# Raw token tiles through the first query and key projections, normalised at the eviction

## The chip, the cores and the metric

The kernel runs on one core of one Trainium2 chip. The metric is the device time of one execution in microseconds (us); lower is better. The core has a matrix engine (PE, whose weight loads are listed as PEld), a vector engine (DVE), a scalar engine (ACT), GpSimd (POOL) and a queue engine (SP) that starts transfers. Transfers run on 16 DMA engines.

## The reference, cut to what matters

```
h  = x + A(layernorm(x))          # attention with a compressive memory, 32 heads of 32
h2 = h + B(layernorm(h))          # gated MLP, 1024 -> 3584 -> 1024
layernorm(x) = (x - mean(x)) / sqrt(var(x) + 1e-5)      # over the 1024 features, no weights
A: q, k, v = n @ wq, n @ wk, n @ wv        # n = layernorm(x), 2048 tokens x 1024
   four segments of 512 tokens; in each: causal softmax attention, plus a read of the memory
   that the earlier segments left; output @ wo
```

All data are bf16. For a token t and an output column o of wq or wk the projection can be written in two ways, which are equal apart from rounding:

```
sum_d (x[t,d] - mean[t]) * r[t] * w[d,o]  =  (sum_d x[t,d]*w[d,o]  -  mean[t] * sum_d w[d,o]) * r[t]
```

with r[t] = (var[t] + 1e-5)^-0.5. The second form needs the column sum of w once, and mean and r of a token only after the product.

## The kernel before, in words

Tokens are worked on in four segments of 512 (four tiles of 128 tokens), features in 8 chunks of 128. A projection of 128 output columns for a segment is a group of 8 matmuls (one for each chunk) into one PSUM bank; there are 8 banks, 0 to 3 shared with the attention scores, 5 to 7 the usual ones of the dense work.

Each engine runs its instructions in an order that is written out: `ORDER` lists for pe, act, dve, pool and sp the numbers of the operations, counted in the order in which the program creates them. `BANKS` gives the first PSUM bank of each group in the order of creation. A group that takes over a bank waits for all operations of the bank's former group, its eviction among them. Waits are derived from what operations read and write; an engine that waits holds everything behind it in its list. A transfer is an entry of the list of the engine that issues it (`sp` for all of them before the change).

The start of the program is `constants` (line 767 on) and `first_half`, for the first segment and the first half (512 columns) of wq, wk and wv:

- `warm` issues matmuls of zeros, 12 at the very start and 5 later, into a bank that nothing reads.
- The loads go out on SP in the list's order: the four token tiles (the first in two halves), then wk's first 256 columns, wq's first 256 columns in two halves of the features, the second 256 columns of wq and of wk, a tile of the next segment, and wv.
- `first_tile` takes a token tile: statistics on DVE (`ln_stats`) or on DVE and ACT (`ln_both`), the deviation by a power on POOL (L880), the scaling on DVE in two halves (L884), four transposes of 128x128 on PE for each half (L719), and a copy of each half from PSUM into `xnT`, the transposed input, on ACT or DVE (`evac`, L730 and L731).
- The projections of the first 256 columns of wq and wk follow tile by tile: 4 groups x 4 tiles x 8 matmuls of 128 columns (L707), each group evicted once. The second 256 columns of wq and wk (`project`) run over 512 columns at once, as do the four groups of wv.
- `attention` begins with ten score passes (L1079, operation 361 is the first), each over banks 0 to 3 and followed by an exponential of 128x2048 on ACT (L1093). Between the passes PE works on projections, those of this segment first and then those of the second half.

Later segments are normalised on the chip and transposed by transposing DMAs (`dma_t`, L395) that SP issues.

Of the kernel before, what the change touches and what calls it, by code (L numbers as in the profile page):

```python
# [8 lines left out]
ALU = mybir.AluOpType  # L9
# [82 lines left out]
    "act": (  # L92
# [473 lines left out]
class Kernel:  # L566
# [305 lines left out]
    def first_tile(self, t):  # L872
# [9 lines left out]
        for b in range(2):  # L882
# [8 lines left out]
            if t == 0 and b:  # L891
                self.warm(5, [self.g.ops[-1]])
# [598 lines left out]
```

## Time and profile before

| | |
|---|---|
| median of 3 runs | 883.78 us (883.63 to 884.16) |
| the profiled execution, its own time | 884.58 us |
| its span, first to last instruction | 882.9 us |
| PE busy | 871.0 us (99% of the span), 5736 instructions |
| DVE, ACT, POOL busy | 438.8, 301.7, 163.0 us |
| read and written in HBM | 84.94 MB and 9.44 MB |

The profile is of one execution. Busy time of an engine is the time that its instructions cover; matmuls are pipelined, so PE counts as busy from a matmul's start until its result stands. The chain of waits follows the work that ended last back to the start. A timeline row merges neighbouring instructions of one kind and gives their start, the time that they cover, their count and the idle time ahead of them.

### The profile page before, as it was taken

To read this page: it belongs to the slowest core of one execution; us is meant where nothing else is said; L and a number is where in the kernel's file an instruction comes from. 1 tells how busy PE (TensorE), PEld (TensorE's weight loads), DVE (VectorE), ACT (ScalarE), POOL (GpSimd) and SP (SyncE) were. 2 spreads that over 40 slices of the span, in tenths; PEclk is the share of its full clock that TensorE was granted. 3 is DMA by queue.
4 is the path that set the end of the run, shared out by engine and by line. 5 is a ranking of instruction groups with operands and counts; after the bars stand their busy time and mean duration, and the time that the engine had idled before them with its cause. 6 is when DMAs were issued, how large, how long until landed. Compare 5 with 4: busy or idle time off the path is not lost.

```text
span 882.9 us, 13660 instructions
## 1 busy us (share of the span) xinstructions
PE 871.0 (99%) x5736; PEld 397.6 (45%) x5825; DVE 438.8 (50%) x735; ACT 301.7 (34%) x345; POOL 163.0 (18%) x226
## 2 busy tenths in 40 slices
PE   8999999999999999999999999999999999999998
PEld 5443444444444444444444444444444444444445
DVE  5787887876666777745354301322243344231011
ACT  4878675768656655511111000111011111110000
POOL 1544344335242444303000000000000000000000
PEclk9999999999999999999999999999999999999999
DMA  7789938555962627395484411211322322201011
GB/s 226 206 191 219 231 100 228 143 145 160 235 156 81 170 66 173 89 289 156 115 242 93 116 36 30 77 55 54 96 73 64 96 72 59 91 7 48 19 42 42
DMA packets 148956, 105.75 MB, mean 120 GB/s; under 512 B 46368, under 2 KB 134688, under 8 KB 147872
## 3 DMA queue, kind: packets, MB, share of 16 engines
q1 hardware_dynamic: 148896, 104.89, 45.5%
q8 instruction: 46, 0.75, 0.4%
q14 instruction: 14, 0.11, 0.0%
HBM read 84.94 MB, written 9.44 MB: 107 GB/s over the span
## 4 chain that ended last, share of the span: by engine, by line
PE 98%; issue 1%; DMA 1%; ACT 0%; SPq 0%; DVE 0%; DVEq 0%
PE ps L707 91%; PE ps L1079 3%; PE ps L1172 3%; DMA wp<-in_A_wk_dram 1%; PE ps L1000 0%; PE ps L1296 0%; SPq L388 0%; ACT et L1093 0%; PE ps L1165 0%; PE ps L719 0%; DVE t L1372 0%; ACT sg L1369 0%; DVE ob L1401 0%; DVEq L524 0%
## 5 line engine op out<-in xcount | busy, mean ns | idle before, releaser
L707 PE MATMUL ps<-hnT,w1b 128*128 128x512 bf16 x881 | 214.5, 379 | 1.1 <-issue 0.5
L707 PE MATMUL ps<-hnT,w3b 128*128 128x512 bf16 x875 | 210.8, 379 | 1.6 <-issue 0.6
L707 PE MATMUL ps<-w2b,hm 128*128 128x512 bf16 (+2 forms) x934 | 198.0, 367 | 1.0
L1369 ACT ACTIVATE sg<-ps 128x512 bf16<-128x512 f32 x112 | 66.8, 597 | 385.5 <-PE ps L707 384.3
L1372 DVE SCALAR_TENSOR_TENSOR t<-sg,ps 128x512 bf16<-128x512 bf16 x112 | 76.7, 686 | 190.5 <-ACT sg L1369 190.2
L1093 ACT ACTIVATE et<-ps 128x2048 bf16<-128x2048 f32 x80 | 150.1, 1876 | 47.7 <-PE ps L1079 45.8
L707 PEld LDWEIGHTS ps<-w2b,hm 128*128 128x128 bf16 x952 | 90.6, 98 | 103.4 <-issue 0.3
L707 PEld LDWEIGHTS ps<-hnT,w1b 128*128 128x128 bf16 x896 | 86.2, 98 | 105.8 <-issue 5.6
L707 PEld LDWEIGHTS ps<-hnT,w3b 128*128 128x128 bf16 x896 | 86.3, 98 | 105.5 <-issue 3.1
L1102 POOL TENSOR_SCALAR_AFFINE_SELECT et<-et 128x512 bf16<-128x512 bf16 (+1 forms) x96 | 83.2, 878 | 112.3 <-ACT et L1093 112.3
L1377 DVE SCALAR_TENSOR_TENSOR hm<-t,ps 128x512 bf16<-128x512 bf16 x112 | 76.2, 684 | 43.5 <-PE ps L707 41.6
L1401 DVE TENSOR_TENSOR ob<-hr,ps 128x512 bf16<-128x512 bf16 (+2 forms) x34 | 21.9, 655 | 122.4 <-PE ps L707 122.3
L707 PE MATMUL ps<-xnT,wp 128*128 128x512 bf16 (+1 forms) x344 | 59.8, 320 | 1.7 <-DMA wp<-in_A_wk_dram 0.8
L707 PE MATMUL ps<-wo,oT 128*128 128x512 bf16 x244 | 59.6, 380 | 1.2 <-issue 0.8
L707 PE MATMUL ps<-hnT,wp 128*128 128x512 bf16 x249 | 58.6, 380 | 0.8 <-issue 0.6
L1118 DVE TENSOR_TENSOR sum<-sum,et 128x512 bf16<-128x512 bf16 (+1 forms) x64 | 40.5, 641 | 6.1 <-POOL et L1102 3.8
L707 PEld LDWEIGHTS ps<-xnT,wp 128*128 128x128 bf16 x352 | 27.9, 98 | 27.3 <-issue 3.5
L707 PEld LDWEIGHTS ps<-wo,oT 128*128 128x128 bf16 x256 | 23.8, 98 | 29.8 <-issue 3.0
L707 PEld LDWEIGHTS ps<-hnT,wp 128*128 128x128 bf16 x256 | 23.5, 98 | 29.7 <-issue 3.7
L1079 PE MATMUL ps<-qT,kT 32*128 32x128 bf16 (+3 forms) x512 | 31.7, 301 | 0.0
L1341 DVE TENSOR_TENSOR h<-h,ps 128x512 bf16<-128x512 bf16 x32 | 21.7, 680 | 20.0 <-PE ps L707 19.6
L707 PE MATMUL ps<-wp,hnT 128*128 128x512 bf16 x124 | 29.8, 380 | 0.4 <-issue 0.3
(101 smaller groups left out, 567.9 us busy)
## 6 DMA issues: line engine op xcount, KB each, us to landing
w1b<-in_B_w_dram SPq DMA_DIRECT2D x28, 512.0 KB, 4.1
w3b<-in_B_w_dram SPq DMA_DIRECT2D x28, 512.0 KB, 4.0
wp<-in_A_wv_dram SPq DMA_DIRECT2D x8, 1024.0 KB, 5.8
wp<-in_A_wq_dram SPq DMA_DIRECT2D x7, 1024.0 KB, 5.4
wp<-in_A_wk_dram SPq DMA_DIRECT2D x7, 1024.0 KB, 7.6
w2b<-in_B_w_dram SPq DMA_DIRECT2D x7, 1024.0 KB, 5.8
h<-in_A_x_dram SPq DMA_DIRECT2D x16, 256.0 KB, 3.0
h_scr<-h SPq DMA_DIRECT2D x16, 256.0 KB, 3.4
```

What stands on the lines that cost most here:

```text
L707: return [e.matmul(p[0](gr), p[1], p[2], start=p[3], stop=p[4]) for p in part]
L1079: ins.append(e.matmul(self.bank(gr, j, 512 - 128 * kc, off), k[r, g0 + g, 128 * kc:128 * kc + 128], q[r, g0 + g, 128 * kc:512], start=True ...
L1093: return [e.activation(et[:, :, :], src, AF.Exp, scale=self.scale)]
L1102: self.pool_op(lambda e, v=v, pat=pat: e.affine_select(v, v, pattern=pat, compare_op=ALU.is_ge, fill=0.0, base=0, channel_multiplier=-1), ...
L1118: lambda e, gr: [e.tensor_tensor(o, a, b, op=ALU.add) for o, a, b in sums],
L1172: ins.append(e.matmul(self.ps[32 * i:32 * i + 32, b * 512 + c0:b * 512 + c0 + n], lhsT(i, kc, j), rhs(i, j), start=kc == 0 and j == first, ...
L1341: self.g.op("dve", dve_ns(512), lambda e, gr, hs=hs: [e.tensor_tensor(hs, hs, self.bank(gr), op=ALU.add)], reads=[hs], writes=[hs], cls=1, ...
L1369: self.g.op("act", act_ns(512), lambda e, gr, sg=sg: [e.activation(sg, self.bank(gr), AF.Tanh, scale=0.5)], writes=[sg], cls=0, group=gg)
L1372: e.scalar_tensor_tensor(t1, sg, 1.0, self.bank(gr), op0=ALU.add, op1=ALU.mult)], reads=[sg], writes=[t1], cls=0,
L1377: e.scalar_tensor_tensor(dst, t1, 0.5, self.bank(gr), op0=ALU.mult, op1=ALU.mult)], reads=[t1], writes=[dst], cls=0,
L1401: self.g.op("dve", dve_ns(n), lambda e, gr, hs=hs, ob=ob, n=n: [e.tensor_tensor(ob, hs, self.bank(gr, 0, n), op=ALU.add)], reads=[hs], wri ...
```

## The change

Tiles 0 to 2 of the first segment are transposed as they arrive and kept as `xr`, with one more column of ones ahead of the tokens (column 1). Six groups, wq's four and wk's first two, are multiplied over `xr`. With the column of ones a group also gets the column sum of its weights. Two of the groups (wq 0 and 1) go tile by tile, 129, 128 and 128 columns; the other four (wk 0 and 1, wq 2 and 3) go over 385 columns in one pass. Tile 3 is normalised first, as all tiles were before; the six groups' columns of tile 3 are multiplied into two banks of their own.

Mean and deviation of the three tiles stand as one column a statistic (`st32`, 128 tokens on the partitions). `spread_rows` transposes them on DVE, writes them to a scratch in DRAM and reads them back onto all 128 partitions as rows (`rows`, 384 KB in all); both transfers are entries of ACT's list. At the eviction of each of the six groups ACT copies the column sum with a minus (csum), DVE adds mean x csum to the bank (scalar_tensor_tensor, 384 columns), and DVE or POOL multiplies by the deviation (tensor_tensor, 384 columns).

The three raw tiles are also normalised in place and transposed by DMA into `xnT`, for wk's groups 2 and 3 and for wv. The warm matmuls are 4 at the start, three after the first tile's transposes. The loads are ordered anew, and wk's first 256 columns come in two halves.

Numbers of the changed kernel that the text uses. Loads: 13, 14 tile 0; 15 tile 1; 18 tile 2; 19 tile 3; 16, 17 wq's first 256 columns by halves of the features; 20, 21 the same of wk; 22 wq's second 256; 23 wk's second 256; 24 wv. Tile 0: 27, 29 transposes; 28, 30 copies; 34 to 37 statistics; 38 power; 39 scaling; 40 transposing DMA. Tile 1: 41 to 44, 45 to 51, 52, 53, 54. Tile 2: 55 to 58, 59 to 62, 63, 64, 65. 66 transposes the statistics, 67 writes them to DRAM, 68 reads the rows. Tile 3: 70 to 76 statistics and power; 77, 80 scaling; 78, 81 transposes; 79, 82 copies. 88 to 99 wq 0 and 1 by tiles; 100 to 107 the passes of 385 columns (wk 0, wk 1, wq 2, wq 3); 108 to 119 tile 3's columns. Eviction, three operations a group (csum, add, multiply): 120 to 122 wq 0; 123 to 125 wq 1; 126 to 128 wk 0; 129 to 131 wk 1; 132 to 134 wq 2; 135 to 137 wq 3. 138, 139 copy tile 3's columns. 140 to 145 wk 2 and 3; 146 to 157 wv's four groups (155, 156 are the last group's matmuls). 379 is the first score pass, 380 its exponential, 382 the second pass. From operation 128 of the kernel before on, the new number is the old one plus 18.

The first lines of the lists, before and after, and the program text:

```diff
     "pe": (
-        "1 30 33-34 86 84-85 87 45 80 48 82-83 81 88 90 94 91 56 89 59 92 95 93 102 100 98 70 99 "
-        "73 103 96-97 104-105 101 108 106 109 107 125 361 110 119 126 111 364 120 116-117 122 "
+        "1 27 29 31-33 41 55 43 88 57 90 89 91 94 92-93 95 98 100 102 96 99 97 106 104-105 101 78 "
+        "81 107 112 103 108 113 109 114 110-111 155 115-119 156 379 152-153 382 149-150 143 394 "
...
     "act": (
-        "38-40 31 35 63 46 64-65 71 112-113 362 115 365 353 377 124 372 139 382 373 371 136 133 "
+        "28 30 47-49 71 67 72-73 123 68 132 79 126 82 120 129 139 135 138 380 383 371 395 145 154 "
...
     "dve": (
-        "0 24-27 37 29 32 50 41-42 51 44 47 52-53 62 49 55 58 66-67 57 60 69 72 74 114 127 "
+        "0 34-37 60 59 42 61 44 62 46 50-51 56 58 66 70 53 39 74-75 77 64 80 124-125 121 130 122 "
+        "127-128 136 133 157 372 214-216 198 151 206 219 207 199 208 385 200 86 386 222-223 402 "
...
     "sp": (
-        "13-15 17 19-20 16 18 21-22 179 23 187 203 369 195 140 153 186 166 194 202 210 360 356 "
+        "14 13 18 15-17 19-20 22 21 24 65 40 54 213 23 197 205 158 221 387 171 184 212 220 228 "
...
 BANKS = (
-    "3013010101567456755566775656676655656756755567567577657576000000000001247300000000000124"
+    "3023331201105674230165567575566756676565675675556756757765757600000000000124730000000000"
...
+    def raw_tile(self, t):
+
+        x = self.xs[t][:, :]
+        for b in range(2):
+            gr = Group([(0,), (1,), (2,)], safe=True)
+            self.transposes(gr, [(c * 128, self.xs[t][:, 512 * b + c * 128:512 * b + c * 128 + 128])
+                                 for c in range(4)], 2)
+            self.evac(gr, self.xr[:, 4 * b:4 * b + 4, 2 + 128 * t:130 + 128 * t], 512,
+                      lambda v: v[:, 0:512].rearrange("p (k n) -> p k n", k=4),
+                      cls=1, bf=True, engs=("dve", "act"))
...
+        mv = self.st32[:, 2 * t:2 * t + 2]
+        rs, mean, op = self.ln_both(t, x, mv) if t % 2 else self.ln_stats(t, x, 1, mv=mv)
...
+        self.dve_op(lambda e: e.tensor_scalar(x, x, mean, rs, op0=op, op1=ALU.mult), 540.0,
+                    [x, mean, rs], [x], 1, port=True)
+        self.g.dma_t(self.xnT[0][:, :, t * 128:(t + 1) * 128], x, 3)
+
+    def spread_rows(self):
+
+        a, b = self.st32[:, :], self.st32t[:, :]
+        self.dve_op(lambda e: e.transpose(b, a), 180.0, [a], [b], 0)
+        sd = self.sd
+        to = bass.AP(sd.tensor, sd.offset, [[32, 4], [128, 32], [1, 32]])
+        of = sd[0:6, :]
+        src = bass.AP(of.tensor, of.offset, [[0, 128], [1, 768]])
...
+        o.emit = lambda e, g: [e.dma_start(to, b)]
...
+        o.emit = lambda e, g: [e.dma_start(rows, src)]
...
-        for t in range(4):
-            self.first_tile(t)
+        for t in range(3):
+            self.raw_tile(t)
+        self.spread_rows()
+        self.first_tile(3)
...
+        more = [(wq, i, Group([(0,), (1,), (2,), (3,)])) for i in (2, 3)]
+        for c0, n in ((1, 129), (130, 128), (258, 128), (1, 385)):
+            for w, i, gr in work[2:] + more if n > 129 else work[:2]:
                 self.g.stage()
+                self.mms(gr, [(lambda gr, c0=c0, n=n: self.bank(gr, 0, n, c0),
+                               w[:, c, i * 128:(i + 1) * 128], xr[:, c, c0:c0 + n],
+                               c == 0, c == 7, n) for c in range(8)], 5, split=4, eager=True)
+        ends = [Group([(0,), (1,), (2,), (3,)]) for w in (wq, wk)]
...
+        for n, (w, i, gr) in enumerate(work + more):
...
+            self.g.op("act", 186.0, lambda e, gr, cs=cs: [e.activation(
+                cs, self.bank(gr)[:, 1:2], AF.Copy, scale=-1.0)], writes=[cs], cls=1, group=gr)
+            self.g.op("dve", dve_ns(384), lambda e, gr, part=part, cs=cs: [e.scalar_tensor_tensor(
+                part, means, cs, self.bank(gr, 0, 384, 2).rearrange("p (t b) -> p t b", t=3),
+                op0=ALU.mult, op1=ALU.add)], reads=[means, cs], writes=[part], cls=1, group=gr)
+            self.either(lambda e, out=out, part=part: e.tensor_tensor(
+                out, part, scales, op=ALU.mult), 384, 2, [scales, part], [out], 1)
```

By `BANKS` the six groups stand in banks 5 (wq 0), 6 (wq 1), 7 (wk 0), 4 (wk 1), 2 (wq 2) and 3 (wq 3), tile 3's columns in banks 0 and 1, and wv's last group (155) takes bank 5.

## Rows read from the trace of the kernel before

**Rows 1.** The page's chain that ended last, shares by engine.

```profile
PE 98%; issue 1%; DMA 1%; ACT 0%; SPq 0%; DVE 0%; DVEq 0%
```

**Rows 2.** Chain in order of time, first 45 us: start, us, what.

```profile
3.13 6.13 DMA wp<-in_A_wk_dram
...
9.30 1.07 PE ps L707 x16
```

**Rows 3.** Timeline of PE, first 20 us: start, us covered, instruction, count, idle before.

```profile
1.24 5.22 PE L707 MATMUL ps<-oT 128*128 128x512 bf16 x12 [1.24 <-DVE oT L772]
6.68 0.72 PE L719 MATMUL ps<-ident,xs 128*128 128x128 bf16 x8 [0.21 <-DVE xs L884]
...
9.30 1.07 PE L707 MATMUL ps<-xnT,wp 128*128 128x128 bf16 x16 [0.83 <-DMA wp<-in_A_wk_dram]
...
18.33 0.39 PE L1079 MATMUL ps<-qT,kT 32*128 32x512 bf16 x4
```

**Rows 4.** Stretches, L707 alone: PE busy, PEld busy, clock, DMA share, GB/s.

```profile
10.88:12.46 1.58, 1.58 (x28) 1.55 (x28) 1.00 1.17 293
```

**Rows 5.** DMA issues at 2.18 and at 3.13 us: KB, us to landing.

```profile
xs<-in_A_x_dram SPq DMA_DIRECT2D x1, 256.0 KB, 4.1
...
wp<-in_A_wk_dram SPq DMA_DIRECT2D x1, 512.0 KB, 6.1
```

**Rows 6.** Timeline of SP, the two issues of Rows 5.

```profile
2.18 0.43 SPq L388 DMA_DIRECT2D xs<-in_A_x_dram  x1
...
3.13 0.43 SPq L388 DMA_DIRECT2D wp<-in_A_wk_dram  x1
```

**Rows 7.** Timeline of all engines: statistics of tile 0's second half.

```profile
3.92 0.69 DVE L834 BATCH_NORM_STATS2 lnst<-xs 128x6 f32<-128x512 bf16 x1 [0.27 <-DMA xs<-in_A_x_dram]
```

**Rows 8.** DVE by line and form: count, busy us, mean ns, idle before.

```profile
L834 DVE BATCH_NORM_STATS2 lnst<-xs 128x6 f32<-128x512 bf16 x28 | 18.4, 674 | 2.1 <-DMA xs<-in_A_x_dram 2.0
...
L837 DVE BATCH_NORM_AGGREGATE lnmv<-lnst 128x2 f32<-128x12 f32 x24 | 4.8, 199 | 0.2
...
L731 DVE COPY xnT<-ps 128x512 bf16<-128x512 bf16 x4 | 1.7, 425 | 2.2 <-PE ps L719 2.2
...
L879 DVE TENSOR_SCALAR lnve<-lnmv 128x1 f32<-128x1 f32 x4 | 0.6, 153 | 0.1
...
L869 DVE TENSOR_SCALAR xs<-xs,lnmv,rstd 128x1024 bf16<-128x1024 bf16 x12 | 7.1, 601 | 2.4 <-POOL rstd L867 2.4
...
L1401 DVE TENSOR_TENSOR ob<-hr,ps 128x512 bf16<-128x512 bf16 x31 | 21.0, 686 | 119.4 <-PE ps L707 119.3
...
L1401 DVE TENSOR_TENSOR ob<-hr,ps 128x256 bf16<-128x256 bf16 x1 | 0.4, 422 | 1.7 <-PE ps L707 1.7
```

**Rows 9.** DMA issues at 231.0, 374.2 and 286.5 us: KB, us to landing.

```profile
r_scr<-T SPq DMA_DIRECT2D x1, 256.0 KB, 2.6
...
r_scr<-T SPq DMA_DIRECT2D x1, 256.0 KB, 5.8
...
R<-r_scr SPq DMA_DIRECT2D x1, 256.0 KB, 4.6
```

**Rows 10.** Tile R0w, read from DRAM onto 32 partitions a transfer: landing of all.

```profile
DMA to landing us min/median/max: 4.7/8.1/9.9
```

**Rows 11.** Timeline of SP: three transposing DMAs in a row, twice.

```profile
35.33 7.17 SPq L395 DMA_TRANSPOSE hnT<-xs  x3
...
80.71 4.54 SPq L395 DMA_TRANSPOSE hnT<-xs  x3
```

**Rows 12.** DMA issues at 24.1 us: KB, us to landing.

```profile
wp<-in_A_wq_dram SPq DMA_DIRECT2D x1, 1024.0 KB, 4.9
```

**Rows 13.** ACT by line and form: the exponential after a score pass.

```profile
L1093 ACT ACTIVATE et<-ps 128x2048 bf16<-128x2048 f32 x80 | 150.1, 1876 | 47.7 <-PE ps L1079 45.8 <-DVE t L1372 0.7 <-issue 0.6
```

**Rows 14.** Who waited for whom on PE, 40 to 120 us: total, times, longest.

```profile
PE ps L707 <- issue: 1.1, 7, 0.2
```

**Rows 15.** Stretch 15 to 20 us: busy us and count of PE, PEld, DVE, ACT, POOL.

```profile
15.00:20.00 5.00, 4.95 (x63) 3.52 (x62) 1.12 (x2) 2.91 (x4) 0.00 (x0) 1.00 0.64 215
```

More of the change, by code (lines that the diff above doesn't have):

```diff
@@ L31 @@
     "pe": (
[60 rows of a table removed]
-    "act": (
[17 rows of a table removed]
-    "dve": (
[38 rows of a table removed]
-    "pool": (
[27 rows of a table removed]
[60 rows of a table added]
+    ),
+    "act": (
[18 rows of a table added]
+    ),
+    "dve": (
[38 rows of a table added]
+    ),
+    "pool": (
[12 rows of a table added]
+    ),
[16 rows of a table added]
+    ),
 }
 BANKS = (
-    "3013010101567456755566775656676655656756755567567577657576000000000001247300000000000124"
-    "7375567655567677566557565665675765000000000001247300000000000012473557676655775676676577"
-    "6560000076755675000000012473000000000000124730000000000001243000000000000124305665575675"
-    "6576575675675675675677565107316576556756756756756401646765645112176123477516566067147512"
-    "6240464765741742104645620164175406601654602543517712717317717447771275715174547354727176"
-    "7543567254614167726564776675635274511652665361546457121514574023412547765765674557405765")
+    "3023331201105674230165567575566756676565675675556756757765757600000000000124730000000000"
+    "0124737556765556767756655756566567576500000000000124730000000000001247355767665577567667"
+    "6577656000007675567500000001247300000000000012473000000000000124300000000000012430566557"
+    "5675657657567567567567567756510731657655675675675675640164676564511217612347751656606714"
+    "7512624046476574174210464562016417540660165460254351771271731771744777127571517454735472"
+    "7176754356725461416772656477667563527451165266536154645712151457402341254776576567455740"
+    "5765"
+)
 HOLD = (
[3 rows of a table removed]
[3 rows of a table added]
 )
@@ L600, in plan @@
         self.beta = buf("beta", [128, 32], BF16)
+        self.mhalf = buf("mhalf", [128, 1], F32)
         self.gcol = buf("gcol", [128, 8], F32)
         self.ocol = buf("ocol", [128, 8], F32)
-        self.mhalf = buf("mhalf", [128, 1], F32)
         self.Mbf = buf("Mbf", [128, 8, 32], BF16)
@@ L644, in plan @@
         self.rd = g.dram("r_scr", [512, 512], F32)
+        raw = self.g.base[self.et[6].name][1]
+        self.xr = buf("xr", [128, 8, 388], BF16, raw)
+        self.rows = buf("rows", [128, 6, 128], F32, raw + 8192)
+        self.part = [buf(f"part{i}", [128, 384], F32, raw + 11264 + 1536 * i) for i in range(2)]
+        self.st32 = buf("st32", [128, 32], F32, raw + 14336)
+        self.st32t = buf("st32t", [128, 32], F32, raw + 14464)
+        self.csum = buf("csum", [128, 8], F32, raw + 14592)
+        self.sd = g.dram("s_scr", [32, 128], F32)
         self.sums = [buf(f"sum{i}", [128, 4, 2, 256], BF16, self.g.base[t.name][1])
@@ L772, in constants @@
         self.dve_op(lambda e: e.memset(w, 0.0), 300.0, [], [w], 0)
-        self.warm(12)
+        self.warm(4)
+        mh = self.mhalf[:, :]
+        P(lambda e: e.memset(mh, -0.5), 1, [], [mh], 0)
         P(lambda e: e.memset(i, 1.0), 128, [], [i], 0)
@@ L776, in constants @@
                                     base=0, channel_multiplier=1), 128, [i], [i], 0)
-        mh = self.mhalf[:, :]
-        P(lambda e: e.memset(mh, -0.5), 1, [], [mh], 0)
         o = self.ones32[:, :, :]
@@ L827, in ln_act, with ln_stats @@
         return sq, nm, ALU.add
-    def ln_stats(self, k, src, cls, deps=()):
+    def ln_stats(self, k, src, cls, deps=(), mv=None):
         self.g.stage()
@@ L835, in ln_stats, with ln_both @@
         st2 = self.lnst[:, k % 16, :].rearrange("p (a b) -> p a b", a=2)
-        mv = self.lnmv[:, k, :]
+        mv = self.lnmv[:, k, :] if mv is None else mv
         self.dve_op(lambda e: e.bn_aggr(mv, st2), 200.0, [st2], [mv], cls)
-        return self.lnmv[:, k, 1:2], self.lnmv[:, k, 0:1], ALU.subtract
-    def ln_both(self, k, src):
+        return mv[:, 1:2], mv[:, 0:1], ALU.subtract
+    def ln_both(self, k, src, mv=None):
         self.g.stage()
@@ L855, in ln_both @@
         parts = st[:, 0:9].rearrange("p (a b) -> p a b", a=3)
-        mv = self.lnmv[:, k, :]
+        mv = self.lnmv[:, k, :] if mv is None else mv
         self.dve_op(lambda e: e.bn_aggr(mv, parts), 200.0, [parts], [mv], 1)
-        return self.lnmv[:, k, 1:2], self.lnmv[:, k, 0:1], ALU.subtract
+        return mv[:, 1:2], mv[:, 0:1], ALU.subtract
     def ln(self, k, src, dst, cls):
@@ L870, in ln @@
                     [src, mean, rs], [dst], cls, port=True)
+    def raw_tile(self, t):
[7 more added lines that the diff above has]
+                      cls=1, bf=True, engs=("dve", "act"))
+            if t == 0 and b:
+                back = self.g.ops[-2]
+                for _ in range(3):
+                    self.warm(1, [back])
+        mv = self.st32[:, 2 * t:2 * t + 2]
+        rs, mean, op = self.ln_both(t, x, mv) if t % 2 else self.ln_stats(t, x, 1, mv=mv)
+        ve, mh = self.lnve[:, t:t + 1], self.mhalf[:, :]
+        self.g.op("dve", 150.0, lambda e, gr: [
+            e.tensor_scalar(ve, rs, self.EPS, None, op0=ALU.add)], reads=[rs], writes=[ve], cls=0)
+        self.g.op("pool", 570.0, lambda e, gr: [e.tensor_tensor(rs, ve, mh, op=ALU.pow)],
+                  reads=[ve, mh], writes=[rs], cls=0)
+        self.dve_op(lambda e: e.tensor_scalar(x, x, mean, rs, op0=op, op1=ALU.mult), 540.0,
[8 more added lines that the diff above has]
+        src = bass.AP(of.tensor, of.offset, [[0, 128], [1, 768]])
+        rows = self.rows[:, :, :].rearrange("p a b -> p (a b)")
+        o = self.g.op("act", 400.0, None, reads=(b,), writes=(sd[:, :],), cls=0, kind="dma")
+        o.bytes = 16384
+        o.emit = lambda e, g: [e.dma_start(to, b)]
+        o = self.g.op("act", 400.0, None, reads=(of,), writes=(rows,), cls=0, kind="dma")
+        o.bytes = 393216
+        o.emit = lambda e, g: [e.dma_start(rows, src)]
     def first_tile(self, t):
@@ L891, in first_tile @@
             if t == 0 and b:
-                self.warm(5, [self.g.ops[-1]])
+                self.warm(1, [self.g.ops[-1]])
             self.evac(gr, out, 512, lambda v: v[:, 0:512].rearrange("p (k n) -> p k n", k=4),
@@ L948, in first_half @@
         loads = [(x0[:, 0:512], y0[:, 0:512]), (x0[:, 512:1024], y0[:, 512:1024]), x[1],
-                 (wq[:, 0:4, 0:256], sq[:, 0:4, 0:256]), x[2],
-                 (wq[:, 4:8, 0:256], sq[:, 4:8, 0:256]), x[3],
-                 (wk[:, :, 0:256], sk[:, :, 0:256]), (wq[:, :, 256:512], sq[:, :, 256:512]),
+                 (wq[:, 0:4, 0:256], sq[:, 0:4, 0:256]), (wq[:, 4:8, 0:256], sq[:, 4:8, 0:256]),
+                 x[2], x[3],
+                 (wk[:, 0:4, 0:256], sk[:, 0:4, 0:256]), (wk[:, 4:8, 0:256], sk[:, 4:8, 0:256]),
+                 (wq[:, :, 256:512], sq[:, :, 256:512]),
                  (wk[:, :, 256:512], sk[:, :, 256:512]), (wv[:, :, :], sv)]
@@ L955, in first_half @@
         self.applied = []
-        for t in range(4):
-            self.first_tile(t)
+        st, one = self.st32[:, :], self.xr[:, :, 1:2]
+        self.pool_op(lambda e: e.memset(st, 0.0), 32, [], [st], 1)
+        self.pool_op(lambda e: e.memset(one, 1.0), 8, [], [one], 1)
+        for t in range(3):
+            self.raw_tile(t)
+        self.spread_rows()
+        self.first_tile(3)
         self.masks(self.applied[-1])
-        x = self.xnT[0]
+        x, xr = self.xnT[0], self.xr
         work = [(w, i, Group([(5,), (6,), (7,), (4,)]))
@@ L961, in first_half @@
                 for w in (wq, wk) for i in range(2)]
-        for c0 in range(0, 512, 128):
-            for w, i, gr in work:
+        more = [(wq, i, Group([(0,), (1,), (2,), (3,)])) for i in (2, 3)]
+        for c0, n in ((1, 129), (130, 128), (258, 128), (1, 385)):
+            for w, i, gr in work[2:] + more if n > 129 else work[:2]:
                 self.g.stage()
-                self.mms(gr, [(lambda gr, c0=c0: self.bank(gr, 0, 128, c0),
-                               w[:, c, i * 128:(i + 1) * 128], x[:, c, c0:c0 + 128],
-                               c == 0, c == 7, 128) for c in range(8)], 5, split=4, eager=True)
@@ L968, in first_half @@
-        for w, i, gr in work:
-            self.g.stage()
-            out = (self.qT if w is wq else self.kT)[0][:, i, :]
-            self.evac(gr, out, 512, lambda b: b, cls=1)
-        for kind, w in (("q", wq), ("k", wk)):
-            for i in (2, 3):
-                self.project(0, kind, 0, i, w)
+                self.mms(gr, [(lambda gr, c0=c0, n=n: self.bank(gr, 0, n, c0),
+                               w[:, c, i * 128:(i + 1) * 128], xr[:, c, c0:c0 + n],
+                               c == 0, c == 7, n) for c in range(8)], 5, split=4, eager=True)
@@ new lines, in first_half @@
+        ends = [Group([(0,), (1,), (2,), (3,)]) for w in (wq, wk)]
+        for w, i, _ in work + more:
+            gr = ends[w is wk]
+            self.g.stage()
+            self.mms(gr, [(lambda gr, i=i: self.bank(gr, 0, 128, 128 * i),
+                           w[:, c, i * 128:(i + 1) * 128], x[:, c, 384:512],
+                           c == 0, c == 7, 128) for c in range(8)], 5, split=4, eager=True)
+        means, scales = (self.rows[:, :, :].rearrange("p (t a) b -> p a t b", a=2)[:, a, :, :]
+                         for a in range(2))
@@ new lines, in first_half @@
+        for n, (w, i, gr) in enumerate(work + more):
+            self.g.stage()
+            out = (self.qT if w is wq else self.kT)[0][:, i, 0:384].rearrange(
+                "p (t b) -> p t b", t=3)
+            cs, part = self.csum[:, n:n + 1], self.part[n % 2][:, :].rearrange(
+                "p (t b) -> p t b", t=3)
+            self.g.op("act", 186.0, lambda e, gr, cs=cs: [e.activation(
[5 more added lines that the diff above has]
+                out, part, scales, op=ALU.mult), 384, 2, [scales, part], [out], 1)
@@ L975, in first_half @@
+        for w, gr, n in ((wq, ends[0], 4), (wk, ends[1], 2)):
+            self.evac(gr, (self.qT if w is wq else self.kT)[0][:, 0:n, 384:512], 128 * n,
+                      lambda b, n=n: b[:, 0:128 * n].rearrange("p (i n) -> p i n", i=n), cls=1)
+        for i in (2, 3):
+            self.project(0, "k", 0, i, wk)
         for i in range(4):
```

279 rows, old and new, of tables (HOLD, ORDER) are left out of this document.

## The prediction

> **What bounds the kernel now.** I read the chain of waits first: PE has 98% of it [rows 1], so apart from the start and the end only PE's own work counts, and a change of the first 30 us is worth what PE's stream starts earlier, less what it later stands still. In the chain's order of time the first piece that is not PE is a load: wk's first 512 KB, issued at 3.13 us, release the first real projection at 9.30 [rows 2]. PE's timeline shows what it did before: 12 warm matmuls from 1.24 us, 0.43 us apart (512 columns at 1.2 GHz), tile 0's eight transposes at 6.68, more warm matmuls, and 0.83 us idle before 9.30 [rows 3]. From 9.30 on the stream has no gap: 28 matmuls of 128 columns take 1.58 us, 0.056 each, the rate of 2.4 GHz [rows 4], and the first score pass stands at 18.33 [rows 3]. So the start is bound by transfers until 9.30 and by PE afterwards.
>
> **When the new stream can start.** The third 256 KB of the loads (a token tile) land at 2.18 + 4.1 = 6.28 us, the first 1536 KB at 3.13 + 6.1 = 9.23 [rows 5, 6]: 256 KB in 0.98 us. In the new order wq's first half is the fourth 256 KB: 6.28 + 0.98 = 7.3 us. Its second half follows at 8.2, tile 3 at 9.2, wk's halves at 10.2 and 13.2, wq's second 512 KB at 12.1, wv at 17.1. The first projection so starts 2.0 us earlier. Behind it stand 12 transposes (tile 2's second half and tile 3) where 24 stood, which saves 12 x 0.056 = 0.67. A pass of 385 columns costs 385/2.4 + 2.6 = 163 ns at the rate of [rows 4] (128 columns: 53.3 + 2.6) against 3 x 56: 32 x 5 ns = 0.16. All other matmuls are as many columns as before, only in another order. Sum: 2.8 us earlier.
>
> Two waits come straight off it. PE wants wq's second half after three pieces of 0.22, at 8.0, and gets it at 8.2 to 8.3; six pieces later, at 9.6, it wants the copy of tile 2's first half. On DVE that copy (56) stands behind thirteen operations: from 3.92 [rows 7] five bn_stats (5 x 0.674), three aggregates (0.60), three small adds (0.46) and two copies (0.85) [rows 8], with about 0.03 between each: 9.6, and the copy itself is done at 10.0. I take 0.3 + 0.4 = 0.7. The stream is then 2.1 us ahead of the old one, if nothing else waits.
>
> **The rows of means and deviations.** This is the new wait. On DVE the transposed statistics (66) come after five bn_stats, three aggregates, three adds and four copies: 3.37 + 0.60 + 0.46 + 1.70 = 6.13 us [rows 8], with 15 steps of 0.03 from 3.92: 10.5. Op 66 is not in the trace; it is between the 0.15 and the 0.69 of the small and the large ops there, and with 32 columns near the small one: 0.2, so 10.7. Then ACT writes 16 KB to DRAM, waits for the landing, and reads 384 KB back. The nearest write landed in 2.6 us, one among heavy traffic in 5.8; the nearest broadcast read of 256 KB in 4.6, and such reads took 4.7 to 9.9 [rows 9, 10]. All of these were issued by SP behind its own loads; no row shows one from ACT. The write could cost 2 us less than the 256 KB did or as much as 5.8, the read 4 to 9.9. I take 2.6, since the 16 KB are less than that row moved, and 4.6, since that read stood among others as large: 10.75 + 2.6 = 13.35, rows at 18.0.
>
> A rule of the Trainium skill bears on the choice: "DMA: Bandwidth & Descriptors", Queues, rings and completion order, says that each DMA engine takes turns between the queues that have work, packet by packet, and that SP and ACT have a queue each. By it the write does not stand behind SP's loads, and 2.6 holds; by the row of 5.8, in the loads' own queue, the sum below would be 3.2 us longer. No run here shows two issuers.
>
> Who waits for the rows: wv's last group (155) takes bank 5 from wq 0, whose bank is free when its add (121) is done, the third op of the eviction on DVE. A DVE op from PSUM takes 0.42 us at 256 columns and 0.69 at 512 [rows 8], 0.55 for 384. So 121 ends at 18.0 + 3 x 0.58 = 19.75. PE reaches 155 at 7.3 + 0.7 + 10.15 = 18.15; the 10.15 are 48 matmuls of 0.056, 12 transposes, 32 passes of 0.163 and 28 end matmuls. Behind 155 everything on PE stands still: **1.6 us**.
>
> Next, the first score pass (379) takes banks 0 to 3, and so waits for the adds of wq 2 and 3, ops eight and nine of that DVE list: 18.0 + 9 x 0.58 = 23.2. PE would be there at 19.8 + 0.86 + 5 x 0.22 + 0.86 = 22.6: **0.6 us**. The second pass (382) stands 8 matmuls (1.73 us) behind the first, whose exponential needs 1.88 us [rows 13] and some 0.5 from pass to pass (0.45 at 18.33, the exponential at 18.78): 2.4 against 0.33 + 1.73: **0.35**.
>
> Sum: -2.1 + 1.6 + 0.6 + 0.35 = **+0.45 us**. The profiled execution took 884.58, a span of 882.9 and 1.7 around it, 0.80 over the median of the runs; its span would become 883.35. For the median: 883.78 + 0.45, **884.2 us**.
>
> **What I cost at nothing.** ACT's six csum copies and two issues (0.2 to 0.4 us each) lie in idle time: ACT had 2.91 us busy of 15 to 20 us [rows 15]. POOL's three multiplies stand after banks are free, POOL being idle in that stretch. Less warm work at the start: at 1.2 GHz PE does about half as much, the nine projection pieces before the copy of tile 2 could take up to 2.0 us more (9 x 0.22); the stream waits 0.7 there and 1.6 at 155 anyhow, and this comes out of those. The ten exponentials start 5 us later and must fit between batches of 12 matmuls, 2.6 + 0.33 us against 2.4: 0.5 of cover a step. Where ACT also evicts in a step, cover is gone; before, PE waited for nothing but issue from 40 to 120 us [rows 14]. Zero to 1 us, I take zero.
>
> **wk's second half on SP.** Its load (23) is moved behind three transposing DMAs and a token load, and SP stands at the first of them (65) until DVE has scaled tile 2 (64). After 66 DVE has one bn_stats, two scalings of 0.60, an aggregate and an add (2.2 us), waits for POOL's power (0.6) and has two more scalings (1.0): 14.9 with the steps between. Three transposing DMAs in a row hold SP 4.5 to 7.2 us [rows 11]: 19.4 to 22.1, the token load 0.4, and the weights 4.9 later [rows 12]: 24.7 to 27.4. PE wants them (143) at 23.2 + 0.33 + 1.73 + 0.35 + 0.33 + 1.73 = 27.7. Just hidden, by the stall at the rows: cost nothing here, and a floor if the rows come early.
>
> **The rivals.** (A) *Rows in time.* If write and read together take under 5.6 us (7.2 here), 155 waits for nothing and the score pass little: -2.1 + 0.35, 882.0. For it: 16 KB and a queue of its own. Against: the broadcast reads never landed under 4.6. (B) *The rows are late: slower.* The write or the read, at the time of the loads of wv, takes the longer of its two ends. With a write of 5.8 us the rows come at 21.2 and all that waits for them moves by 3.2: +3.65, 887.4. It turns slower by more than 0.2% when the rows land after 19.3 us. For it: the DMA engines are full in that stretch (a share of 1.17 [rows 4]) and the loads to come are as many. Against it: 16 KB is little, and the row of 5.8 stood behind other loads of its queue. (C) *wk's second half is the later of the two.* It needs rows in time and the slow transposes; 143 is then reached at 25.5 and waits up to 27.4: -1.75 + 1.9 = +0.15, 883.9.
>
> **How the numbers follow.** Forecast 0.42 (883.0 to 885.9), A 0.25 (881.2 to 882.7), B 0.22 (885.9 to 889), C 0.11 (882.7 to 885.9). The runs shown lie within 0.5 us; 0.2%, 1.77 us, is about what can be told from no change. Faster, under 882.0: two thirds of A, 0.16. Slower, over 885.55: B, and 0.07 of the forecast and C, 0.29. Between: 0.55. The range leaves out a third of A and the later half of B: 881.8 to 887.6.
>
> **What would show it.** The first projection at 7.3 +- 0.4 us instead of 9.30. On ACT a transfer issued near 10.8, the next near 13.4, and DVE's first add near 18. PE idle before wv's last group, released by DVE's add from bank 5, and again before the first score pass, which stands near 23.3 instead of 18.33. Wrong if PE has no gap at bank 5, if the weights of wk 2 and 3 release PE, or if PE idles between later score passes, which I cost at nothing.

## The result and the profile after

The changed kernel takes 888.03 us (median of 6 runs, 886.54 to 889.17) against 884.50 for the kernel before beside it (6 runs, 883.63 to 884.86): a ratio of 1.0042, 95% interval [1.0029, 1.0055]. It is slower by 3.5 us. The forecast was 884.2 in a range of 881.8 to 887.6, with 0.55 for no measurable change and 0.29 for slower: the likeliest case was the wrong one, and the time is 0.4 us outside the range.

The profiled execution is the lowest of the six: 886.54 us with a span of 884.5, which is 1.96 us more than the profiled execution of the kernel before took (884.58). Its PE timeline answers to [rows 3] (start, us covered, instruction, count, idle before):

```profile
1.24 1.89 PE L724 MATMUL ps<-oT 128*128 128x512 bf16 x4 [1.24 <-DVE oT L789]
3.64 1.03 PE L736 MATMUL ps<-ident,xs 128*128 128x128 bf16 x8 [0.51 <-DMA xs<-in_A_x_dram]
...
5.99 0.84 PE L736 MATMUL ps<-ident,xs 128*128 128x128 bf16 x12 [0.44 <-DMA xs<-in_A_x_dram]
6.84 0.40 PE L724 MATMUL ps<-xr,wp 128*128 128x129 bf16 x4
...
7.84 6.37 PE L724 MATMUL ps<-xr,wp 128*128 128x129 bf16 x64 [0.15 <-DMA wp<-in_A_wq_dram]
...
15.81 0.40 PE L724 MATMUL ps<-xnT,wp 128*128 128x128 bf16 x4 [0.50 <-ACT csum L1048]
...
16.71 1.50 PE L724 MATMUL ps<-xnT,wp 128*128 128x128 bf16 x24
20.82 0.81 PE L724 MATMUL ps<-wp,xnT 128*128 128x512 bf16 x3 [2.61 <-DVE part L1050]
...
23.91 0.40 PE L1164 MATMUL ps<-qT,kT 32*128 32x512 bf16 x4 [0.31 <-DVE part L1050]
```

The first projection stands at 6.84 us (9.30 before). At 18.2 PE has done all that it can do and stands still for 2.61 us until DVE's add frees bank 5 (below, "the stall"); it stands again for 0.31 before the first score pass, at 23.91 (18.33 before). The chain in order of time, which answers to [rows 2], names what holds the add (start, us, what):

```profile
9.11 0.21 DVE st32t L917
9.32 0.03 DVE lnst L865
9.35 5.33 DMA s_scr<-st32t
14.68 0.02 issue
14.70 4.00 DMA rows<-s_scr
18.70 0.02 issue
18.72 0.63 DVE part L1050
```

From ACT's issue of the 16 KB write to its issue of the read, which waits for the write, it is 5.35 us (5.33 in the chain); the read takes 4.00. Laid side by side, the exponentials of the score passes are 5.58 us later than before at the first and 1.02 later from 62 us on; the difference of 4.56 is order: projections that stood between the passes now stand ahead of them (a kernel without the stall has it too, below). The 1.02 stay up to 280 us. Then the offset becomes 1.83, by an idle time of PE that the kernel before did not have (below, "the pause"):

```profile
281.73 1.48 PE L1257 MATMUL ps<-et,v 128*32 128x512 bf16 x36
283.86 0.51 PE L1257 MATMUL ps<-et,v 128*32 128x384 bf16 x12 [0.65 <-issue]
```

Nothing that the profile shows ends this wait; the work on both sides of it is one operation, the same as before. Four of the six executions have a mean granted clock of 0.998 (887.73 to 889.17 us), the other two, the profiled one among them, 1.0 (886.54 and 887.87); every execution of the kernel before has 1.0.

So there are three suspects: the rows (write and read) and the stall that they cause; what a stall does to PE's clock; the pause at 283 us.

### The profile page after: what moved, and what is told of

It is laid out like the page before. It is cut to its first block, busy times and chain, and to the rows that moved or that the text cites. A ratio compares the mean times of both kernels' runs of the same rounds, so it can differ in the third digit from the quotient of the medians.

```text
span 884.5 us, 13635 instructions
## 1 busy us (share of the span) xinstructions
PE 868.4 (98%) x5710; PEld 397.1 (45%) x5799; DVE 444.9 (50%) x741; ACT 300.3 (34%) x348; POOL 166.4 (19%) x231
## 4 chain that ended last, share of the span: by engine, by line
PE 96%; DMA 1%; DVE 1%; issue 1%; ACT 0%; SPq 0%; DVEq 0%
PE ps L724 89%; PE ps L1164 3%; PE ps L1257 3%; DMA s_scr<-st32t 1%; DMA rows<-s_scr 0%; ACT et L1178 0%; DVE part L1050 0%; DMA xs<-in_A_x_dram 0%; PE ps L1085 0%; PE ps L1381 0%; DVE lnst L851 0%; PE ps L1250 0%; DVE xr L748 0%; DVE qT L1053 0%; DVE t L1457 0%
## 5 line engine op out<-in xcount | busy, mean ns | idle before, releaser
L1187 POOL TENSOR_SCALAR_AFFINE_SELECT et<-et 128x512 bf16<-128x512 bf16 (+1 forms) x96 | 80.9, 855 | 102.5 <-ACT et L1178 102.5
L724 PE MATMUL ps<-xnT,wp 128*128 128x512 bf16 (+1 forms) x249 | 50.7, 349 | 1.3 <-issue 0.6
L724 PEld LDWEIGHTS ps<-xnT,wp 128*128 128x128 bf16 x256 | 22.0, 98 | 25.4 <-issue 2.8
L724 PE MATMUL ps<-wp,xnT 128*128 128x512 bf16 x123 | 29.4, 379 | 2.9 <-DVE part L1050 2.6
```

The lines of the kernel that those rows point to most:

```text
L724: return [e.matmul(p[0](gr), p[1], p[2], start=p[3], stop=p[4]) for p in part]
L1187: self.pool_op(lambda e, v=v, pat=pat: e.affine_select(v, v, pattern=pat, compare_op=ALU.is_ge, fill=0.0, base=0, channel_multiplier=-1), ...
```

## Experiments

Each was timed beside the kernel before on the same chip, in three batches in which that one took 884.40, 884.56 and 884.72 us.

| kernel | us, median (range, runs) | ratio to before [95%] | runs at clock 0.998 |
|---|---|---|---|
| e0 the change again | 887.70 (886.40 to 889.03, 5) | 1.0038 [1.0025, 1.005] | 2 |
| e1 rows constant | 883.58 (882.76 to 884.10, 11) | 0.9989 [0.998, 0.9998] | 0 |
| e2 gap filled | 886.52 (885.98 to 887.55, 10) | 1.0024 [1.0015, 1.0033] | 0 |
| e3 rows made by PE | 883.64 (882.89 to 884.40, 11) | 0.999 [0.9981, 0.9999] | 0 |
| e4 e3, wk's load earlier | 883.82 (882.64 to 884.91, 11) | 0.9991 [0.9982, 1.0] | 0 |
| e5 e3, more warm work | 883.12 (882.78 to 883.92, 11) | 0.9983 [0.9974, 0.9992] | 0 |
| e6 e3, 23 small matmuls | 882.75 (882.17 to 883.25, 11) | 0.9979 [0.997, 0.9988] | 0 |
| e7 wv's load later | 888.98 (1) | | 1 |
| e9 the change, 23 small matmuls | 887.50 (886.00 to 888.32, 5) | 1.0032 [1.002, 1.0044] | 3 |
| e10 before, 23 small matmuls | 885.60 (884.11 to 888.80, 12) | 1.0019 [1.0009, 1.0029] | 2 |

**e0: the changed kernel again.** No edit.

> The changed kernel once more, beside the three below. Its six runs so far spread from 886.54 to 889.17 us, and four of them show a mean granted clock of 0.998 where the kernel before shows 1.000 over its span. Theory 1 (the rows' round trip through DRAM, with PE's 2.6 us gap at bank 5, is the whole loss): 887 to 888 us, and the clock has nothing to do with the spread. Theory 2 (the same gap also lets the clock fall to 1.2 GHz in most executions, which costs some 1 to 2 us more): again 886.5 to 889, the lower times where the clock is 1.000.

It is slower by as much as the first time. In this execution tile 0 came later (transposes at 4.10 us), the write took 5.14 and the read 4.57, and the first add was at 19.97; PE's stall:

```profile
21.84 1.02 PE L724 MATMUL ps<-wp,xnT 128*128 128x512 bf16 x4 [2.97 <-DVE part L1050]
```

From 62 us on it is 2.27 behind the kernel before, where the first profile was 1.02 behind: the start varies by over a microsecond from one execution to the next. One reason stands in the trace. PE works at 1.2 GHz until 9.6 us here, until 5 to 6 us in the first profile; twelve transposes that took 0.84 us there take

```profile
6.21 1.49 PE L736 MATMUL ps<-ident,xs 128*128 128x128 bf16 x12
```

**e1: the rows without the trip through DRAM.** The rows are filled with ones long before they are needed, so the kernel leaves out the means and deviations of tiles 0 to 2; all other work stays.

```diff
-        (write of st32t to DRAM, read back onto 128 partitions, both on ACT)
+        self.pool_op(lambda e: e.memset(rows, 1.0), 768, [], [rows], 1)
```

> The two transfers of the rows are taken away: a memset of ones on POOL, long before, stands for the means and deviations of tiles 0 to 2, which are left out; all else is as in the changed kernel. Both theories: PE's gap before wv's last group (2.6 us) goes and the first score pass comes at about 21 us instead of 23.9; the span in the early part is 1.9 us under the kernel before. Theory 1: about 1.5 to 3 us faster than before the change on the same chip. Theory 2 adds that all runs have a clock of 1.000 and lie within 0.6 us of each other, and that the gain over the changed kernel is 4 to 5 us, more than the gap. Rival (the run-to-run part comes from the fewer warm matmuls at the start): the spread of 2 us and 0.998 stay. Rival (wk's second half is then late): a gap of 1 us or more appears before wk's third and fourth group.

No stall at bank 5, the score pass at 21.97, and the whole 4.1 us below the change beside it. The trip and what follows from it are worth all of the loss. All eleven executions have a mean clock of 1.0 although the start has the few warm matmuls of the change, so these are not what lowers it. Less was gained over the kernel before than either theory said (0.8 us instead of 1.5 to 3), and the executions still spread over 1.34 us, not 0.6: in the profiled one PE reaches 2.4 GHz only at 9.85 us and its lead at 62 us is 0.92 instead of 1.9, and a pause of 0.3 (at 281 us) is still there.

**e2: the stall filled.** 23 zero matmuls of 256 columns into an unused half of bank 1, in an operation shortly ahead of the stall.

```diff
+                o.emit = lambda e, gr, real=real: real(e, gr) + [
+                    e.matmul(self.bank(gr, 0, 256, 256), z[:, 4, 0:128], z[:, 4, 0:256],
+                             start=True, stop=True) for _ in range(23)]
```

> The changed kernel with 23 matmuls of zeros (256 columns, into the unused half of bank 1) placed where PE would stand still ahead of wv's last group: PE waits as long for the rows, but is busy for all but some 0.2 us of it. Theory 2: the time of the changed kernel's best runs, 886.5 (+-0.7), with a clock of 1.000 in all runs: 1 to 2 us under the changed kernel's median. Theory 1, or the start as the cause of 0.998: no difference to the changed kernel, 887.5 to 888.5, spread as wide.

The filling, and what the score pass still waits for:

```profile
17.35 2.67 PE L1044 MATMUL ps<-oT 128*128 128x256 bf16 x23
19.86 1.06 PE L724 MATMUL ps<-xnT,wp 128*128 128x128 bf16 x16
...
24.08 0.40 PE L1170 MATMUL ps<-qT,kT 32*128 32x512 bf16 x4 [0.31 <-DVE part L1056]
```

The rows come no sooner (first add at 18.88), yet the time falls by 1.2 us and no execution has 0.998. But this kernel also has no pause at 283 us, so one edit did two things; e9 parts them.

**e3: the rows made by PE.** DVE multiplies the identity by each statistic (128x768, 0.96 us), PE sums over the partitions with a matrix of ones, ACT copies the two banks. The products are in bf16, where the trip through DRAM carried 32-bit values.

```diff
+        self.dve_op(lambda e: e.tensor_tensor(dg[:, :, :], eye, col, op=ALU.mult), 950.0, ...)
+            e.matmul(self.bank(gr, 0), one, flat[:, 0:512], start=True, stop=True),
+            e.matmul(self.bank(gr, 1, 256), one, flat[:, 512:768], start=True, stop=True)],
+        self.g.op("act", 830.0, lambda e, gr: [e.activation(rows, ..., AF.Copy)], ...)
```

> The rows are made without a transfer: DVE multiplies the identity by the six columns of statistics (128x768, in bf16), PE multiplies a square of ones by that (512 and 256 columns, banks 0 and 1), ACT copies the 768 columns to the rows. Rows at about 12 us instead of 18.7. Both theories: no gap at bank 5, first score pass at about 21 us; as fast as the kernel without the transfers within 0.5 us (0.3 us more on PE), so 1 to 3 us under the kernel before and 4 to 5 under the changed one if theory 2 holds, 2 to 3 under the changed one if only theory 1 does.

ACT has the rows at 12.3 us instead of 18.7, and PE goes through without a stall:

```profile
11.44 0.81 ACT L930 ACTIVATE rows<-ps 128x768 f32<-128x768 f32 x1 [1.18 <-PE ps L927]
```

```profile
16.53 1.50 PE L725 MATMUL ps<-xnT,wp 128*128 128x128 bf16 x24
17.86 1.03 PE L725 MATMUL ps<-wp,xnT 128*128 128x512 bf16 x4
...
20.92 0.40 PE L1170 MATMUL ps<-qT,kT 32*128 32x512 bf16 x4
```

From 62 us on it is 1.97 us ahead of the kernel before: the prediction gave the stream 2.1 with the rows in time. Of the whole only 0.8 is left, at the lower end of what was expected or under it (1 to 3). At the first pass it is 2.58 behind: 4.55 of order, as in the change. Of the lead 0.19 goes at about 178 us, and 1.02 at 280 us, in the pause:

```profile
278.94 1.47 PE L1263 MATMUL ps<-et,v 128*32 128x512 bf16 x34
281.04 0.56 PE L1263 MATMUL ps<-et,v 128*32 128x512 bf16 x10 [0.63 <-issue]
```

**e4: e3 with wk's second half ahead of the transposing DMAs on SP.**

```diff
-        "14 13 18 15-17 19-20 22 21 24 65 40 54 213 23 197 ...
+        "14 13 18 15-17 19-20 22 21 24 23 65 40 54 213 197 ...
```

> The kernel whose rows TensorE makes, with the load of wk's second half put back ahead of the three transposing DMAs on SP. Theory: in the kernel without it wk 2 and 3 are reached at about 25 us and its load lands just about then, so that at most 0.3 us is won: 883.2 to 883.7. Rival C of the prediction (wk's second half is the floor once the rows are early): TensorE stops before wk 2 in the kernel without it, and the time falls by 0.5 to 1.9 us. Against both: tile 2's normalised copy comes 3 us later by the load, nobody waits for it before 40 us: no loss.

1.95 ahead at 62 us, as e3: no gain. Rival C's floor isn't there, even with the rows early.

**e5: e3 with PE kept at work at the start.**

```diff
-        self.warm(4)
+        self.warm(6)
-                for _ in range(3):
-                    self.warm(1, [back])
+                for n in (1, 1, 2):
+                    self.warm(n, [back])
```

> The kernel whose rows TensorE makes (883.64 us there), with three more warm matmuls of 512 columns at the start: six in the first batch instead of four, and one more after tile 0's transposes, so that TensorE has no hole of 0.8 us at 2.8 us and the first transposes stand later by nothing (they wait for tile 0 anyway). Theory S (the late rise of the clock at the start costs part of the time): the short spacing of the matmuls begins by 6 to 7 us instead of 9 to 10, the projections before it run up to 2 us sooner, and the time falls by 0.5 to 1.5 us, to 882.1 to 883.1. Rival (the stream waits for the loads and for the copies of tiles 2 and 3 there in any case): the rise is earlier and the time is the same within 0.3 us. The pause of 0.65 to 1.0 us at 283 us should be there in both, since only three matmuls are added (if it is the place in TensorE's instruction fetch that sets it), or be changed.

The matmuls of 128 columns go from 0.107 to 0.056 us apart, from 1.2 to 2.4 GHz, at 4.0 us, in e3 at 7.6. But the score pass comes no sooner (21.23): the stream waits for loads and copies there, as the rival said. The time falls by 0.5 us all the same (0.7 against e4, timed beside it), and the trace shows where a part of it comes from: the pause is no longer at 280 us. There is one of 0.48 at 178 instead, and behind both places e5 is 1.03 ahead of the kernel before, e3 0.77:

```profile
178.32 0.18 PE L1091 MATMUL ps<-v,pkn 128*32 128x33 bf16 x1 [0.48 <-issue]
```

**e6: e3 with 23 zero matmuls of 48 columns behind the first four warm ones.**

```diff
+        small = [(lambda gr: self.bank(gr, 0, 48), z, w[:, 0:48], True, True, 48)] * 23
-                           512)] * n, 0, split=n)
+                           512)] * n + (small if n == 4 else []), ...)
```

> The kernel whose rows TensorE makes (883.64 us there), with 23 zero matmuls of 48 columns behind the first four warm ones: about 1 us of work in a stretch where TensorE has a hole, and all later matmuls 23 places further in its instruction stream (as many as the run that filled the gap had, which had no pause at 283 us). Theory F (the pause of 0.65 to 1.0 us at 283 us comes from where a fetch of instructions falls among the matmuls): no pause there, the later score passes keep the lead of 2.0 us that they have at 62 us over the kernel before instead of losing 1.2, and the time is 882.4 to 882.9. Rival (the pause is something of the work at 283 us itself, such as a transfer or a buffer): the pause stays and the time is 883.3 to 883.9.

No pause at 280 us, one of 0.27 at 177, a lead of 1.76 kept to the attention's end, and 882.75 us: the best of all, 1.8 us under the kernel before and some 5 under the change. (0.24 of what it gains over e3 is made at the start, where its clock rises at 6.0 us instead of 7.6.) The work in which e3 paused is the same here, so it isn't that work; 3 or 23 more matmuls ahead move the pause. e0, e1 and e3 have it behind the same matmul of the recorded stream (number 2619), at 284.2, 280.9 and 280.0 us. In the first profile of the change, one packet of an instruction queue falls between 280 and 284 us:

```profile
q8 instruction: 1, 0.02, 2.3%
```

That makes the fetch of PE's instructions the likely cause. All nine pauses in the profiles of these runs agree: such a packet has ended 0.8 to 1.1 us before PE stops, and PE goes on 1.35 to 1.6 us after its end, whether the pause is 0.27 or 0.65 long. It is still argued, not shown: some 46 such packets fall into a profile, and at most two of them have a pause behind them.

**e7: is it the queue?** In the change, from 9.4 to 13.6 us, while ACT's write is issued and not landed, the packets by queue (q1 is SP's, q10 ACT's) are:

```profile
DMA packets 1739, 1.35 MB, mean 320 GB/s; under 512 B 33, under 2 KB 1739, under 8 KB 1739
## 3 DMA queue, kind: packets, MB, share of 16 engines
q1 hardware_dynamic: 1739, 1.35, 110.5%
```

and from 13.6 to 15 us:

```profile
q1 hardware_dynamic: 246, 0.14, 34.8%
q10 hardware_dynamic: 132, 0.02, 7.6%
```

Not one packet of ACT's queue moves before 13.6 us, when SP's loads ebb. The same holds in e0, e2 and e9: the write is issued at 9.9 to 10.2 us there and its first packets come at 13.4 to 13.75, so not its issue sets the time but the loads. Now wv's load, the last of them, was moved behind a transposing DMA:

```diff
-        "14 13 18 15-17 19-20 22 21 24 65 40 54 213 23 197 ...
+        "14 13 18 15-17 19-20 22 21 65 24 40 54 213 23 197 ...
```

> The changed kernel with the load of wv (1 MB, the last of the eight bulk loads) moved behind the first transposing DMA in SP's order, so that it is issued at 12 to 14 us instead of 5; nothing else is changed. Theory W (the write of the statistics on ACT's queue stands until SP's bulk loads have run out): the loads that are left run out at 10.5 to 11 us, the write's packets begin then instead of at 13.7, and it lands at 11 to 12.5, 2 to 3 us after its issue instead of 5.3. Rival (a write of 128 pieces to DRAM from ACT takes 5.3 us from its issue, whatever else is loaded): it lands at 14.5 to 15 as before. The time of the whole rises or stays in both, since the projections with wv then wait for the load (landing at 17 to 18 us).

ACT's two issues in this kernel (start, us, engine line op, tiles) and the packets from 9.9 to 12 us:

```profile
9.93 1.09 ACTq L925 DMA_DIRECT2D s_scr<-st32t  x1
...
11.96 0.34 ACTq L928 DMA_DIRECT2D rows<-s_scr  x1
```

```profile
GB/s 283 264 302 283 322 283 293 273 234 254 254 254 254 254 195 166 166 146 88 20 20 29 20 20 37 63 63 54 54 56 32 315 0 0 0 0 0 0 0 0
...
q10 hardware_dynamic: 132, 0.02, 5.1%
```

The loads ebb at 11 us (40 slices of 0.05 us), the write's packets go then, and the read can be issued 2.03 us after the write instead of 5.35. The write is short in itself; what it stood behind are SP's loads. (One execution, but the rival's landing at 14.5 to 15 us is ruled out by a read issued at 11.96.) The whole is no faster, since wv's weights then hold PE for 3.68 us. That longer stall shows the second suspect:

```profile
21.63 1.46 PE L724 MATMUL ps<-wp,xnT 128*128 128x512 bf16 x3 [3.68 <-DMA wp<-in_A_wv_dram]
22.89 2.32 PE L724 MATMUL ps<-xnT,wp 128*128 128x128 bf16 x20
```

```profile
20.00:25.00 5.00, 3.37 (x23) 2.65 (x25) 0.96 (x2) 0.45 (x2) 0.27 (x1) 0.66 1.08 282
```

In this stretch (PE, PEld, DVE, ACT, POOL busy, granted clock, DMA share, GB/s) the granted clock is 0.66. After the stall the 20 matmuls of 128 columns take 2.32 us where the change needs 1.28: they are 0.107 us apart, 1.2 GHz, from 21.63 to 25.02. This execution's mean clock is 0.998, as that of four of the first six of the change.

**e9: the change with the 23 small matmuls, the stall left.**

> The changed kernel with the 23 zero matmuls of 48 columns at the start and nothing in the gap before wv's last group: what the run that filled the gap had of two things at once (23 more matmuls in the stream, and the gap filled) is here the first alone. The changed kernel stood at 887.7 to 888.0, the one with the gap filled at 886.5. Theory of two parts: the pause at 283 us goes (0.7 to 0.8 us), the gap of 2.6 to 3 us stays and with it executions with a mean granted clock of 0.998: 886.8 to 887.3, half of them or more at 0.998. Rival P (the pause alone made the difference of 1.2 us): 886.3 to 886.6 and every execution at 1.0. Rival G (the gap and the clock alone made it): 887.5 to 888.1.

The median, 887.50, is above what the theory of two parts gave (886.8 to 887.3) and at the edge of rival G, but the executions part by clock. At 1.0 they take 886.29 us on average (2), at 0.998 887.90 (3); those of the change, both batches together, 887.19 (5) and 888.58 (6). So the shift is worth 0.9 and 0.7 us (there is no pause at 283 here), and the clock 1.6 and 1.4. e2, with both, has 886.64 on average, all at 1.0: as far as two executions of e9 can tell, filling the stall took away the low clock and nothing else. With few executions each of these has an error of some tenths; that both parts exist is likely by the times, and the traces of e2 and e9, without the pause, support it. The profile, of one at 0.998, shows the low clock behind the stall at the rows, until 24.4 us: 2.95 us of work at half the rate cost some 1.5, as much as the times part by:

```profile
21.45 1.49 PE L724 MATMUL ps<-wp,xnT 128*128 128x512 bf16 x3 [2.95 <-DVE part L1051]
22.73 2.05 PE L724 MATMUL ps<-xnT,wp 128*128 128x128 bf16 x20
```

```profile
20.00:25.00 5.00, 3.55 (x25) 2.68 (x27) 4.24 (x8) 0.62 (x3) 1.60 (x2) 0.66 1.01 293
```

**e10: the control.** The kernel before with the small matmuls behind its twelve warm ones.

> A control: the kernel before with the same 23 zero matmuls of 48 columns behind its twelve warm ones, 0.5 to 0.9 us of work that ends before wk's first half lets the first projection go. If a pause depends on where the instructions stand, one of 0.3 to 1 us may appear anywhere in this kernel or none, and the time moves with it: 884.0 to 885.5, the trace showing the same difference at one place. If the pauses belong to the changed kernel's work, the time stays within 0.2 us of the kernel before.

Neither theory holds. Two executions of twelve have 0.998 (888.8 us), and those at 1.0 reach from 884.11 to 887.33, wider than any other kernel here. The profile is of the lowest one, 0.30 ahead of the kernel before from 285 us on, and so shows nothing of the loss. No profile shows the two at 0.998, and this kernel does not have the new stall: a low clock can have another cause too. Such filling at the start is thus not harmless everywhere; why it costs this kernel 0.9 us and not e6 stays open.

## Why the prediction was wrong, point by point

- **The start: right, in part by luck.** First projection forecast at 7.3, measured 6.84 (7.49 in e0); waits of 0.7 forecast, 0.15 for wq's second half and none for the copy of tile 2, but 0.50 for a copy that stands on ACT behind the read's issue (costed at nothing: csum and issues lie in idle time, but ACT stood 3.50 us for the write's landing). PE reaches wv's last group at 18.2; forecast 18.15. It began 0.46 earlier and its work took 0.6 longer than the 10.15 forecast.
- **The transposed statistics: 1.4 us too late.** Their operation was forecast to start at 10.5 and started at 9.11 behind the same fifteen operations. DVE began 0.3 us earlier, and the mean durations of [rows 8] overstate the step from one instruction to the next: a copy of 0.425 is followed after 0.33, a bn_stats of 0.674 after 0.60.
- **The write: the step that failed.** "I take 2.6, since the 16 KB are less than that row moved." It took 5.33 (5.14, 4.82 and 4.80 in e0, e2 and e9): the price of the row of 5.8 [rows 9], rival B's. Bytes were the wrong measure; what counts here is what is queued when it is issued. The Trainium skill, "DMA: Bandwidth & Descriptors", Queues, rings and completion order, has each DMA engine take turns between its queues packet by packet. By that rule the write would not have stood behind SP's loads; the trace differs, 1739 packets to none over 4.2 us (ACT's issue itself takes the first 1.1 of them), and the measurement decides. Whether the write had work in its queue all that time no profile shows.
- **The read: 4.00, forecast 4.6.** Rows at 18.70, forecast 18.0: -1.4, +2.7 and -0.6. The earlier statistics hid most of the miss, and that is luck.
- **The stalls: right in place, larger in size.** 2.61 against 1.6 at bank 5, where both the place and the releaser were as named; 0.31 against 0.6 at the score pass (23.91 against 23.2); none of the 0.35 at the second. After the ten passes +1.02 in the profiled execution, against +0.45, and +2.27 in e0. Given when the rows come, the sum was right: moved with them from 18.0 to 18.70 and 19.94, its +0.45 becomes +1.15 and +2.39.
- **Nothing for the clock after a stall: wrong, the second step that failed.** The prediction spoke of less warm work at the start and gave no term and no reason for the new stall. Six of eleven executions of the change pay 1.4 us for it, 0.8 on the average.
- **Nothing behind 60 us: wrong by 0.5 to 0.9**, the pause at 283 us. The prediction named idle time between later score passes as a sign of being wrong, and this is one, but not for the reason that it thought of (evictions on ACT). No row of before could tell it.
- **wk's second half: right,** hidden, and hidden without the stall too (e4).

The miss of 3.8 us then is: 0.7 that the kernel before itself stands higher here (884.50 against 883.78); about 1.2 of rows and stall (e9 at clock 1.0 is 1.6 over the kernel before beside it, forecast 0.45); 0.8 of clock; 0.8 of pause. That sums to 3.5; what remains is within the error of these averages. Rival B had the write's price, but that its 887.4 comes near the time is luck: in it the rows come at 21.2, the measured ones came at 18.70, for which the same sum gives 884.9. The rest is the clock, the pause and the kernel before, none of which B had.

## What to carry to other kernels

Price a small transfer that something waits for by what is queued ahead of it on all queues, not by its bytes: where the rows of before have a fast and a slow landing, look at which stretch the new one falls into. To put a few columns onto all partitions as rows in a stretch full of loads, a diagonal and a matmul with ones (0.96 us on DVE, some 0.3 on PE, 0.81 on ACT) went around the DMA engines and turned a loss of 3.5 us into a gain of 0.8. A new stall of PE of this length (2.6 to 3 us) costs its length and, in about half of the executions here, some 1.5 us more for the clock behind it.

## What the runs showed that was not expected

- A queue of its own did not help a small write: ACT's first packet came over 4.2 us after the issue, when SP's bulk loads ebbed, and 1.2 us after it with fewer loads ahead (e7). Which rule the DMA engines follow, by age or by queue, no run here tells.
- Behind the stall of 2.6 to 3 us about half of the executions have a mean granted clock of 0.998, and the one profiled among them (e9) runs at 1.2 GHz there, for some 3 us; filled with zero matmuls (e2) it stayed at 2.4 in all ten.
- A pause of PE of 0.3 to 0.65 us sits at one place of the instruction stream, 260 us behind the change; three more matmuls at the start move it, at 0.5 to 1 us of the whole time. Each pause begins 0.8 to 1.1 us after a packet of an instruction queue has ended. Two kernels that differ by such a number of instructions can't be compared closer than that without a look for it.
